# Retention states in a fused attention and MLP kernel: one scan per head pair instead of a chain of multiply-adds, with a new order of the first stage

## The chip, the cores and the metric

The kernel runs on one core of a Trainium2 chip. The metric is the device time of one execution in microseconds (us). The span of a profile is some 2 us shorter than the time of the same execution, and a profile is one execution: where it and the median of several differ, the median decides whether a kernel is faster, and the profile says where the time lies.

## The reference, cut to what matters

Four batches, 8 heads, 768 tokens, 64 elements per head. Retention keeps a 64x64 state per head, which decays by a constant gamma of that head:

```
for t in range(S):
    state = gamma * state + outer(k[t], v[t])
    y[t]  = scale * q[t] @ state
```

Its output, as 768 x 512, goes through a Fourier transform along both axes (real part), a layer norm and two dense layers (512 to 2048, relu, back to 512), with residual sums:

```
u   = x + real(fft(fft(x, axis=1), axis=2))
un  = (u - mean) / sqrt(var + 1e-6)
out = u + relu(un @ w1) @ w2
```

## The kernel before

Retention works on pairs of heads (128 partitions) and six chunks of 128 tokens. Each chunk's output has two parts. Mask products are the scores within the chunk, multiplied by a decay mask on VectorE, times v. State outputs are q times the state left by the earlier chunks. The state after chunk c is gamma^128 times the one before plus the state product kᵀv of the chunk. This is how the states are made (a matmul line of 128 x 128 holds both heads, of which the diagonal 64 x 64 blocks are used):

```python
s16 = sp.tile([P, NCH - 1, P], f16, tag="s16", name="s16")
for c0, n in ((0, 3), (3, 2)):
    wk = ps_g.tile([P, 3, P], f32, ...)                       # PSUM
    for c in range(c0, c0 + n):
        nc.tensor.matmul(wk[:, c - c0, :], kd[:, c]..., v16[:, c]..., start=True, stop=True)
    for c in range(c0, c0 + n):
        if c == 0:
            ...copy s16[:, 0] <- wk[:, 0]   # ScalarE in batch one, VectorE later
        else:
            nc.vector.scalar_tensor_tensor(out=s16[:, c], in0=s16[:, c - 1],
                scalar=gk128[:, hp:hp + 1], in1=wk[:, c - c0], op0=ALU.mult, op1=ALU.add)
```

And this is how they are used; both groups add into the same PSUM tile, state outputs first:

```python
for c in range(1, NCH):
    for h2 in range(2):
        ...lhsT = qT..., rhs = s16[..., c - 1, sl]             # 64 elements that lie together
        nc.tensor.matmul(yk[h2][:, c, :], lhsT, rhs, start=(c == 1), stop=False, ...)
for h2 in range(2):
    for c in range(NCH):
        nc.tensor.matmul(yk[h2][:, c, :], atm[:, c, h2, :], v16[:, c, h2, :], ..., stop=(c == NCH - 1))
```

Later batches' retention is interleaved with the dense layers of the batch before, so that TensorE always has large matmuls between the small ones.

## Time and profile before

| | before |
|---|---|
| median of 3 runs | 275.0 us (274.45 to 275.61) |
| span of the profile, granted clock | 273.1 us, 0.994 |
| first matmul of the first dense layer | 42.69 us |
| first and last matmul of the second dense layer | 58.36 and 268.74 us: a stretch of 210.4 us |
| state outputs in that stretch, start to start | 29 ns where they stand together; in batch two, where each uses 64 rows of TensorE, 29 ns for two, which run side by side |

The "stretch": what comes before it is the first stage, in it TensorE is almost full (busy for 201.6 of the 210.4 us in this trace). A line of a timeline has start, length, then what.

Second, TensorE's timeline (start, length, then what), at the first matmuls of the two dense layers:

```profile
42.69 4.72 PE L573 MATMUL psh<-unT,w 128*128 128x128 f16 x64
...
58.36 1.03 PE L593 MATMUL psc<-w,ht 128*128 128x512 f16 x4
```

And VectorE's, where the third batch's first pair ends. Links of the state chain and masks alternate there, and a link is last: the last state is done 1.0 us after the last mask. So it is in 13 of the 16 pairs of this trace: the last state comes after the last mask.

```profile
121.14 0.68 DVE L319 TENSOR_TENSOR atm<-wkA,maskp 128x512 f16<-128x512 f32 x1
121.74 0.34 DVE L345 SCALAR_TENSOR_TENSOR s<-s,gk,wkK 128x128 f16<-128x128 f16 x1
...
122.46 0.33 DVE L345 SCALAR_TENSOR_TENSOR s<-s,gk,wkK 128x128 f16<-128x128 f16 x1
```

### The profile page before, as it was taken

Reading aid. Unit: us, or ns where it says so; the run is one execution under the profiler, and the core shown is the slowest. Engines: PE = TensorE matmul, PEld = TensorE weight load, DVE = VectorE, ACT = ScalarE, POOL = GpSimd, SP = SyncE. Lnnn points to the kernel's source line nnn. Section 1 sums busy time; section 2 is a strip of 40 time slices with the busy share of each in tenths; the row PEclk is TensorE's granted clock in tenths of the full one; section 3 lists DMA queues with packets and bytes.
Section 4 is the critical chain, followed back from the end, with each engine's and each line's share of the span. In section 5 each row is a group of like instructions: output and inputs, shape, how many; then the busy total and the mean of one; then the engine's idle time right before and its main releaser. Section 6 shows DMA issues by size and latency. Waiting matters only on the chain.

```text
span 273.1 us, 5125 instructions
## 1 busy us (share of the span) xinstructions
PE 243.8 (89%) x1972; PEld 147.7 (54%) x1972; DVE 179.8 (66%) x458; ACT 116.6 (43%) x238; POOL 71.9 (26%) x122
## 2 busy tenths in 40 slices
PE   1498569998999998889999899989999999999994
PEld 0375458964456453556556544665566445545541
DVE  8964954986677676789778662699687736623411
ACT  3887456665554333546424540452234405402300
POOL 5769002565211214134402220510001303100000
PEclk9999997999999999999999999999999999999999
DMA  8999996999999597958996022144310131112012
GB/s 184 263 245 152 204 204 143 250 245 231 195 202 178 127 211 170 226 111 164 219 212 138 2 49 97 48 106 70 114 41 0 38 97 41 38 58 79 0 38 77
DMA packets 97432, 35.97 MB, mean 132 GB/s; under 512 B 88193, under 2 KB 94337, under 8 KB 97409
## 3 DMA queue, kind: packets, MB, share of 16 engines
q1 hardware_dynamic: 93184, 31.47, 54.2%
q0 software_dynamic: 4224, 4.19, 9.5%
q8 instruction: 15, 0.25, 0.4%
q14 instruction: 9, 0.07, 0.1%
HBM read 27.26 MB, written 6.29 MB: 123 GB/s over the span
## 4 chain that ended last, share of the span: by engine, by line
PE 56%; DVE 23%; ACT 7%; POOL 5%; issue 5%; DMA 1%; POOLq 0%; ACTq 0%; DVEq 0%
PE psc L593 25%; PE psh L556 14%; DVE bst L510 4%; PE ps L432 3%; POOL u L500 3%; PE wkY L366 2%; DVE u L491 2%; POOL u L497 2%; DVE xab L395 2%; PE tq L278 2%; PE psh L573 2%; PE wkY L370 2%; PE wkA L299 2%; DVE ht L562 2%; DVE ob L597 1%
## 5 line engine op out<-in xcount | busy, mean ns | idle before, releaser
L593 PE MATMUL psc<-w,ht 128*128 128x512 f16 x384 | 90.4, 379 | 0.7 <-DVE ht L562 0.7
L556 PE MATMUL psh<-unT,w 128*128 128x384 f16 x448 | 84.0, 326 | 0.9 <-ACT ht L560 0.5
L593 PEld LDWEIGHTS <-ht 128*128 128x128 f16 x384 | 36.0, 98 | 38.4 <-issue 2.0
L556 PEld LDWEIGHTS <-w 128*128 128x128 f16 x448 | 41.6, 98 | 27.4 <-issue 4.6
L560 ACT ACTIVATE ht<-psh 128x384 f16<-128x384 f32 x56 | 27.3, 489 | 61.6 <-PE psh L556 61.6
L562 DVE TENSOR_SCALAR ht<-psh 128x384 f16<-128x384 f32 x56 | 30.6, 547 | 11.8 <-PE psh L556 11.7
L597 DVE SCALAR_TENSOR_TENSOR ob<-psc,stats,u 128x512 f32<-128x512 f32 x24 | 17.9, 746 | 29.0 <-PE psc L593 29.0
L497 POOL TENSOR_TENSOR u<-u,x 128x256 f32<-128x256 f32 x18 | 11.5, 637 | 91.9 <-DVE u L491 89.5
L253 POOL TENSOR_SCALAR kd<-k,gexp 128x384 f16<-128x384 f32 x32 | 19.6, 623 | 30.6 <-DMA k<-in_k_dram 14.3
L512 ACT ACTIVATE un<-u,stats 128x512 f16<-128x512 f32 x21 | 15.1, 721 | 22.9 <-DVE stats L511 22.2
L378 ACT ACTIVATE x<-wkY,gexp 128x384 f16<-128x384 f32 x32 | 17.0, 585 | 16.8 <-PE wkY L370 16.7
L302 DVE SCALAR_TENSOR_TENSOR atm<-wkA,maskf 128x384 f16<-128x384 f32 x32 | 16.9, 547 | 8.7 <-PE wkA L299 8.6
L345 DVE SCALAR_TENSOR_TENSOR s<-s,gk,wkK 128x128 f16<-128x128 f16 x64 | 21.6, 338 | 0.5
L510 DVE BATCH_NORM_STATS2 bst<-u 128x6 f32<-128x512 f32 x21 | 14.6, 694 | 10.1 <-POOL u L500 9.9
L366 PE MATMUL wkY<-s,qTz 64*128 64x64 f16 (+1 forms) x160 | 16.6, 204 | 4.2 <-DVE s L345 2.9
L366 PEld LDWEIGHTS <-qTz 64*128 64x128 f16 (+1 forms) x160 | 10.7, 100 | 14.5 <-issue 9.8
L500 POOL TENSOR_TENSOR u<-u,x 128x256 f32<-128x256 f32 x21 | 13.6, 650 | 16.9 <-DVE u L493 15.7
L258 POOL TENSOR_SCALAR v<-v 128x768 f16<-128x768 f32 x16 | 13.3, 834 | 17.1 <-DMA v<-in_v_dram 7.0
L491 DVE SCALAR_TENSOR_TENSOR u<-pq,g,qn 128x257 f32<-128x257 f32 x24 | 11.5, 479 | 7.4 <-ACT qn L488 7.4
L319 DVE TENSOR_TENSOR atm<-wkA,maskp 128x512 f16<-128x512 f32 x24 | 16.3, 681 | 0.1
L573 PE MATMUL psh<-unT,w 128*128 128x128 f16 x192 | 12.7, 228 | 0.0
L573 PEld LDWEIGHTS <-w 128*128 128x128 f16 x192 | 12.2, 104 | 0.4 <-issue 0.2
(110 smaller groups left out, 294.3 us busy)
## 6 DMA issues: line engine op xcount, KB each, us to landing
q<-in_q_dram SPq DMA_DIRECT2D x16, 384.0 KB, 5.2
k<-in_k_dram SPq DMA_DIRECT2D x16, 384.0 KB, 4.9
v<-in_v_dram SPq DMA_DIRECT2D x16, 384.0 KB, 5.9
out_dram<-ob SPq DMA_DIRECT2D x24, 256.0 KB, 2.2
w<-in_moe_w_ch_dram POOLq DMA_DIRECT2D x8, 512.0 KB, 10.8
unT<-un SPq DMA_TRANSPOSE x12, 2.4
qTz<-q16z SPq DMA_TRANSPOSE x8, 3.8
kT<-kd SPq DMA_TRANSPOSE x8, 2.8
```

Source lines behind the costliest of these rows:

```text
L253: kc = nc.gpsimd.tensor_scalar(out=kd[:, :, h2, :], in0=k32[:, h2], scalar1=gkd[:, h0 + h2:h0 + h2 + 1], scalar2=1.0, op0=ALU.mult, op1=AL ...
L345: nc.vector.scalar_tensor_tensor(out=s16[:, c], in0=s16[:, c - 1], scalar=gk128[:, hp:hp + 1], in1=wk[:, c - c0], op0=ALU.mult, op1=ALU.add)
L366: nc.tensor.matmul(yk[h2][:, c, :], lhsT, rhs, start=(c == 1), stop=False, skip_group_check=True)
L378: nc.scalar.activation(dst, yk[h2], AF.Copy, bias=0.0, scale=gq8[:, h:h + 1])
L500: eng.tensor_tensor(out=u[:, kb, 256:512], in0=u[:, kb, 256:512], in1=x[:, kb, 1, 257:1:-1], op=ALU.add)
L510: nc.vector.bn_stats(bst, u[:, kb, :])
L556: nc.tensor.matmul(psh, w116[:, cb, fb * P:(fb + 1) * P], unT[:, cb, rt * 384:(rt + 1) * 384], start=(cb == 0), stop=(cb == 3))
L560: nc.scalar.activation(ht16[:, fb, :], psh, AF.Relu, bias=0.0, scale=-1.0)
L562: nc.vector.tensor_scalar(out=ht16[:, fb, :], in0=psh, scalar1=-1.0, scalar2=0.0, op0=ALU.mult, op1=ALU.max)
L573: nc.tensor.matmul(psh[:, f], w116[:, cb, fb * P:(fb + 1) * P], unT[:, cb, kb * P:(kb + 1) * P], start=(cb == 0), stop=(cb == 3))
L593: nc.tensor.matmul(psc, ht16[:, fb, rb3 * P:(rb3 + 1) * P], w216[:, fb, :], start=(fb == 0), stop=(fb == NFB - 1))
L597: nc.vector.scalar_tensor_tensor(out=ob, in0=psc, scalar=lb[b]["st"][:, rb, 3:4], in1=lb[b]["u"][:, rb, :], op0=ALU.mult, op1=ALU.add)
```

## The change

The intent: all five states of a pair by one VectorE scan (out[i] = data0[i] * out[i-1] + data1[i]). For that, the five values of one state element must lie side by side, so the products are written to PSUM with the chunk innermost, and data0 is a table of gamma^128 with zeros wherever a new element starts. A product is now made per head, as two matmuls of 64 output partitions each (column tiles), so that no unused blocks are scanned. The mask products come first and the state outputs after them, one head after the other where the two heads alternated before. The table takes room in SBUF, which is found by letting the cast queries of the first two batches share a buffer with the padded queries of the later ones; the zeroing of its padding moves from the start to the end of batch one. In the first stage the pairs are ordered so that the left half of the columns is done after two pairs, the folds that feed the transform come as soon as their heads are done, and transposes of the next pair stand ahead of the current pair's outputs. The core of the diff, with cuts:

```diff
-PAIR_ORDER = [0, 3, 1, 2]
+PAIR_ORDER = [0, 1, 3, 2]
...
+        nc.vector.tensor_copy(gk5[:, hp], gk128[:, hp:hp + 1].unsqueeze(2).to_broadcast([P, D, NCH - 1]))
+    nc.vector.memset(gk5[:, :, :, 0], 0.0)
...
-            s16 = sp.tile([P, NCH - 1, P], f16, tag="s16", name="s16")
-            ... two PSUM tiles, five matmuls of 128 columns, one copy, four multiply-adds
+            s16 = st["s16"] = sp.tile([P, D, NCH - 1], f16, tag="s16", name="s16")
+            wkf = ps_g.tile([P, D * (NCH - 1)], f32, tag="g", name="wkK", padded_shape=[P, DM])
+            wk = wkf.rearrange("p (e c) -> p e c", c=NCH - 1)
+            for c in range(NCH - 1):
+                for h2 in range(2):
+                    nc.tensor.matmul(wk[64 * h2:64 * h2 + 64, :, c], kd[:, c, h2, :],
+                                     v16[:, c, h2, :], start=True, stop=True)
+            nc.vector.tensor_tensor_scan(
+                out=s16.rearrange("p e c -> p (e c)"),
+                data0=gk5[:, hp].rearrange("p e c -> p (e c)"),
+                data1=wkf, initial=0.0, op0=ALU.mult, op1=ALU.add)
...
-            ... state outputs, rhs = s16[..., c - 1, sl], then mask products
+            ... mask products, then state outputs, rhs = s16[..., :, c - 1]
...
     def first_units():
-        un = []
+        un = [cast_unit(0, 0), tp_unit(0, 0, 0), tp_unit(0, 0, 1)]
         for i in range(4):
-            un += [cast_unit(0, i), t_unit(0, i), a0_unit(0, i, 0), kv_unit(0, i), a0_unit(0, i, 1)]
+            ... cast and transposes of pair i + 1 between a0_unit and kv_unit of pair i
...
+            if i == 1:
+                un.append(fold_s(0, 0, 258, 0, 1))
```

More of the change, by code (lines that the diff above doesn't have):

```diff
@@ L53 @@
     inp = pool("inp", 11)
-    qp = pool("qp", 2)
     vp = pool("vp", 4)
@@ L80 @@
     epsT = const.tile([P, 1], f32, tag="epsT")
-    gk128 = const.tile([P, NHP], f32, tag="gk128")
+    gk5 = const.tile([P, NHP, D, NCH - 1], f32, tag="gk5")
     pmask = const.tile([P, 4], f32, tag="pmask")
@@ L143 @@
                             scalar2=None, op0=ALU.mult)
+    gk128 = const.tile([P, NHP], f32, tag="gk128")
     for hp in range(NHP):
@@ L146 @@
         nc.vector.memset(gk128[64:128, hp:hp + 1], float(gam[2 * hp + 1] ** P))
+        nc.vector.tensor_copy(gk5[:, hp], gk128[:, hp:hp + 1].unsqueeze(2).to_broadcast(
+            [P, D, NCH - 1]))
+    nc.vector.memset(gk5[:, :, :, 0], 0.0)
     nc.gpsimd.memset(hpi, float(np.pi / 2))
@@ L154, in late_consts, with pad_unit @@
                                      scale=float(gam[h] ** (-P)))
+    def pad_unit():
         for j in range(2):
@@ L242, in run @@
                         es.enter_context(tc.issue_after(last_cast[b, i - 1].ins))
-                    q16 = qp.tile([P, NCH, 2, D], f16, tag="q16", name="q16")
+                    q16 = qzs[i % 2].rearrange("p c h t -> p (c h t)")[:, 0:NCH * P].rearrange(
+                        "p (c h d) -> p c h d", c=NCH, h=2)
                     es.enter_context(tc.issue_after(nc.gpsimd.tensor_scalar(
@@ L262, in cast_unit, with tp_unit, run @@
         return run
+    def tp_unit(b, i, part):
+        def run():
+            if part == 0:
+                at[b, i] = dict(
+                    kT=tp.tile([P, NCH, P], f16, tag="kT", name="kT"),
+                    qT=qts[i % 2].rearrange("p c h t -> p (c h) t")[:, 0:NCH])
+            st = at[b, i]
+            src = (q16_of, kd_of)[part][b, i]
+            tq = ps_g.tile([P, NCH, P], f16, tag="g", name="tq", padded_shape=[P, 8, P])
+            for c in range(NCH):
+                nc.tensor.transpose(tq[:, c, :], src[:, c].rearrange("p a b -> p (a b)"), ident16)
+            if part == 0:
+                nc.scalar.copy(st["qT"].rearrange("p c t -> p (c t)").rearrange(
+                    "p (t c) -> p t c", c=NCH), tq.rearrange("p c t -> p t c"))
+            else:
+                nc.scalar.copy(st["kT"], tq)
+        return run
@@ L264, in t_unit @@
     def t_unit(b, i):
         def run():
+            if b < NPE:
+                tp_unit(b, i, 0)()
+                tp_unit(b, i, 1)()
+                return
             st = at[b, i] = {}
             kT = st["kT"] = tp.tile([P, NCH, P], f16, tag="kT", name="kT")
-            if b >= NPE:
-                qT = st["qT"] = qts[i % 2]
-                nc.sync.dma_start_transpose(qT.rearrange("p c h t -> p (c h) t"),
-                                            q16_of[b, i].rearrange("p c h d -> p (c h d)"))
-                nc.sync.dma_start_transpose(kT, kd_of[b, i].rearrange("p c h d -> p (c h d)"))
-                return
@@ L274, in run @@
-            qT = st["qT"] = qts[i % 2].rearrange("p c h t -> p (c h) t")[:, 0:NCH]
-            for dst, src in ((qT, q16_of[b, i]), (kT, kd_of[b, i])):
-                tq = ps_g.tile([P, NCH, P], f16, tag="g", name="tq", padded_shape=[P, 8, P])
-                for c in range(NCH):
-                    nc.tensor.transpose(tq[:, c, :], src[:, c].rearrange("p a b -> p (a b)"),
-                                        ident16)
-                if dst is qT:
-                    nc.scalar.copy(dst.rearrange("p c t -> p (c t)").rearrange(
-                        "p (t c) -> p t c", c=NCH), tq.rearrange("p c t -> p t c"))
-                else:
-                    nc.scalar.copy(dst, tq)
+            qT = st["qT"] = qts[i % 2]
@@ L285, in t_unit @@
+            nc.sync.dma_start_transpose(qT.rearrange("p c h t -> p (c h) t"),
+                                        q16_of[b, i].rearrange("p c h d -> p (c h d)"))
+            nc.sync.dma_start_transpose(kT, kd_of[b, i].rearrange("p c h d -> p (c h d)"))
         return run
@@ L329, in run @@
             kd, v16 = kd_of[b, i], v16_of[b, i]
-            s16 = sp.tile([P, NCH - 1, P], f16, tag="s16", name="s16")
-            st["s16"] = s16
-            for c0, n in ((0, 3), (3, 2)):
-                wk = ps_g.tile([P, 3, P], f32, tag="g", name="wkK", padded_shape=[P, 4, P])
-                for c in range(c0, c0 + n):
-                    nc.tensor.matmul(wk[:, c - c0, :], kd[:, c].rearrange("p a b -> p (a b)"),
-                                     v16[:, c].rearrange("p a b -> p (a b)"),
-                                     start=True, stop=True)
-                for c in range(c0, c0 + n):
-                    if c == 0:
-                        if b == 0:
-                            nc.scalar.copy(s16[:, 0], wk[:, 0])
-                        else:
-                            nc.vector.tensor_copy(s16[:, 0], wk[:, 0])
-                    else:
-                        nc.vector.scalar_tensor_tensor(out=s16[:, c], in0=s16[:, c - 1],
-                                                       scalar=gk128[:, hp:hp + 1],
-                                                       in1=wk[:, c - c0],
-                                                       op0=ALU.mult, op1=ALU.add)
+            s16 = st["s16"] = sp.tile([P, D, NCH - 1], f16, tag="s16", name="s16")
[9 more added lines that the diff above has]
+                data1=wkf, initial=0.0, op0=ALU.mult, op1=ALU.add)
         return run
@@ L358, in run @@
                   for _ in range(2)]
-            for c in range(1, NCH):
-                for h2 in range(2):
-                    sl = slice(64 * h2, 64 * h2 + 64)
-                    if b < NPE:
-                        lhsT, rhs = qT[sl, c, :], s16[sl, c - 1, sl]
-                    else:
-                        lhsT, rhs = qT[:, c, h2, :], s16[:, c - 1, sl]
-                    nc.tensor.matmul(yk[h2][:, c, :], lhsT, rhs,
-                                     start=(c == 1), stop=False, skip_group_check=True)
             for h2 in range(2):
@@ L370, in run @@
                     nc.tensor.matmul(yk[h2][:, c, :], atm[:, c, h2, :], v16[:, c, h2, :],
-                                     start=False, stop=(c == NCH - 1), skip_group_check=True)
+                                     start=(c == 0), stop=False, skip_group_check=True)
+            for h2 in range(2):
+                sl = slice(64 * h2, 64 * h2 + 64)
+                for c in range(1, NCH):
+                    if b < NPE:
+                        lhsT, rhs = qT[sl, c, :], s16[sl, :, c - 1]
+                    else:
+                        lhsT, rhs = qT[:, c, h2, :], s16[:, :, c - 1]
+                    nc.tensor.matmul(yk[h2][:, c, :], lhsT, rhs, start=False,
+                                     stop=(c == NCH - 1), skip_group_check=True)
                 h = 2 * hp + h2
@@ L645, in first_units @@
     def first_units():
-        un = []
+        un = [cast_unit(0, 0), tp_unit(0, 0, 0), tp_unit(0, 0, 1)]
         for i in range(4):
-            un += [cast_unit(0, i), t_unit(0, i), a0_unit(0, i, 0), kv_unit(0, i), a0_unit(0, i, 1)]
+            nxt = i < 3
+            if nxt:
+                un += [cast_unit(0, i + 1)]
+            un += [a0_unit(0, i, 0)]
+            if nxt:
+                un += [tp_unit(0, i + 1, 0)]
+            un += [kv_unit(0, i), a0_unit(0, i, 1)]
+            if nxt:
+                un += [tp_unit(0, i + 1, 1)]
             if i == 3:
-                un += [fold_s(0, 0, 130, 0, 2), fold_s(0, 130, 258, 0, 1), fold_d(0, 0),
-                       g0_unit(0), s1_unit(0, 0, 0), s1_unit(0, 1, 0)]
+                un += [fold_s(0, 0, 130, 1, 2), fold_d(0, 0), g0_unit(0), s1_unit(0, 0, 0),
+                       s1_unit(0, 1, 0)]
             un.append(y_unit(0, i))
+            if i == 1:
+                un.append(fold_s(0, 0, 258, 0, 1))
             if i < 3:
@@ L656, in first_units @@
                 un.append(parity_consts)
-        un += [xmean_unit(0), fold_s(0, 130, 258, 1, 2), fold_d(0, 1), s1_unit(0, 0, 1),
-               s1_unit(0, 1, 1), xmean_unit(1), xmean_unit(2), mean_unit]
+        un += [fold_s(0, 130, 258, 1, 2), fold_d(0, 1), s1_unit(0, 0, 1), s1_unit(0, 1, 1),
+               xmean_unit(0), xmean_unit(1), xmean_unit(2), mean_unit]
         return un
@@ L716 @@
             streams.append((mix_units(b + 1, [0, 1, 2]), b + ts[-1], b + ts[-1] + 0.15))
+    streams.append(([pad_unit], 0.9, 0.95))
     emit(streams)
```

## The prediction

> **What bounds the kernel now.** I read the page first, then the stages, then the matmuls of one stage in order of time, then the first stage engine by engine.
>
> The page's busy time (first block), then busy time by stage (us from the start; busy us and count of each engine, granted clock, DMA share, GB/s):
>
> ```profile
> PE 243.8 (89%) x1972; PEld 147.7 (54%) x1972; DVE 179.8 (66%) x458; ACT 116.6 (43%) x238; POOL 71.9 (26%) x122
> ```
> ```profile
> 20.00:30.00 10.00, 7.72 (x88) 5.27 (x87) 5.60 (x15) 6.53 (x14) 7.27 (x11) 1.00 1.09 171
> ...
> 180.00:210.00 30.00, 29.79 (x270) 18.72 (x269) 24.68 (x63) 10.45 (x22) 1.23 (x2) 1.00 0.30 69
> 210.00:240.00 30.00, 28.64 (x160) 15.38 (x159) 17.28 (x40) 11.15 (x24) 7.39 (x12) 1.00 0.18 49
> ```
>
> There are two regimes. From about 62 us on TensorE is nearly full, so an instruction counts there only by the TensorE time it takes or makes TensorE wait. Before 43 us no engine is full: it is a chain of loads, casts, copies and small vector operations for the first batch, ending when the first dense layer starts at 42.7 us.
>
> The groups the change touches (busy us, mean ns of one, idle before and its releaser):
>
> ```profile
> L345 DVE SCALAR_TENSOR_TENSOR s<-s,gk,wkK 128x128 f16<-128x128 f16 x64 | 21.6, 338 | 0.5
> ...
> L302 DVE SCALAR_TENSOR_TENSOR atm<-wkA,maskf 128x384 f16<-128x384 f32 x32 | 16.9, 547 | 8.7 <-PE wkA L299 8.6
> L319 DVE TENSOR_TENSOR atm<-wkA,maskp 128x512 f16<-128x512 f32 x24 | 16.3, 681 | 0.1
> ...
> L366 PE MATMUL wkY<-s,qTz 64*128 64x64 f16 x80 | 9.1, 215 | 1.7 <-DVE s L345 1.7
> ...
> L335 PE MATMUL wkK<-v,kd 128*128 128x128 f16 x80 | 8.3, 241 | 0.0
> ...
> L366 PE MATMUL wkY<-s,qTz 128*128 128x64 f16 x80 | 7.5, 192 | 2.6 <-DVE s L345 1.2 <-DVE s L343 0.8 <-DVE unT L543 0.2
> ```
>
> The second batch (64 to 74 us, TensorE's timeline) shows what pieces cost, from start to start:
>
> ```profile
> 63.36 0.82 PE L593 MATMUL psc<-w,ht 128*128 128x512 f16 x3
> 64.11 0.20 PE L366 MATMUL wkY<-s,qTz 64*128 64x64 f16 x1
> 64.24 0.39 PE L593 MATMUL psc<-w,ht 128*128 128x512 f16 x1
> ...
> 69.74 0.44 PE L335 MATMUL wkK<-v,kd 128*128 128x128 f16 x5
> 70.02 1.03 PE L593 MATMUL psc<-w,ht 128*128 128x512 f16 x4
> ...
> 73.33 0.52 PE L370 MATMUL wkY<-v,atm 128*128 128x64 f16 x12
> 73.69 1.24 PE L593 MATMUL psc<-w,ht 128*128 128x512 f16 x5
> ```
>
> Twelve L370 take 0.36 us, 30 ns each with a 128-column weight load in it. Five L335 take 0.28 us, 56 ns each. In long runs L593 comes every 0.216 us, so three are 0.65; here the next start, a matmul of 64 rows, is at 0.75: 0.10 us lost on entering the 64-row form. It then takes 0.13 us instead of 0.03: 0.10 lost on leaving. State by state, as VectorE delivers them, these matmuls are scattered between large ones.
>
> The first stage, last pair of heads (ACT copies the transposed key, PE multiplies, DVE masks and makes states):
>
> ```profile
> 25.16 0.80 ACT L284 COPY kT<-tq 128x768 f16<-128x768 f16 x1
> ```
> ```profile
> 26.01 0.39 PE L299 MATMUL wkA<-qTz,kT 64*128 64x128 f16 x4 [0.72 <-ACT kT L284]
> ...
> 30.97 0.24 PE L366 MATMUL wkY<-s,qTz 64*128 64x64 f16 x2 [0.50 <-DVE s L345]
> ...
> 33.40 1.13 PE L432 MATMUL ps<-csp,eo 128*128 128x193 f16 x6
> ...
> 37.23 0.64 PE L482 MATMUL pq<-cd,g 128*128 128x257 f16 x2
> ```
>
> POOL, second batch's second pair:
>
> ```profile
> 55.64 1.15 POOL L253 TENSOR_SCALAR kd<-k,gexp 128x384 f16<-128x384 f32 x2 [0.73 <-DMA k<-in_k_dram]
> ```
>
> This key is cast at 56.8 us, straight behind its load, and TensorE transposes it at 58.0: 1.2 us of slack, which limits what an earlier start can bring.
>
> [...]
>
> **The change part by part.**
>
> States. Removed per pair: five matmuls of 128 columns (0.28 us) and the chain of four L345 plus one copy. From start to start an L345 takes about 0.25 us, so the chain costs VectorE some 1.2 us, and spread among other work it took 3.3 us for the pair at 63 us. Added: ten matmuls with 64 output partitions and 64 columns, written every fifth fp32, and one scan of 320 elements. The mask rows above give the full rate: 512 elements take 681 ns, 384 take 547, so 1.05 ns per element. [...] The larger effect is on waits: TensorE's waits in front of L366 from 62 us on add up to some 3.5 us. Not all go, as the mask products are now needed first and VectorE still finishes them after the scan. I count 2.5: 0.5 in batch two, 2.0 in three and four.
>
> State products. At the rate of L370 ten would again take 0.29 us[...]. Then the mode: batches three and four have no switches now and get two per pair, 8 x 2 x 0.10 = 1.6 us. In batch two the new instruction order has its state products in one run instead of among large ones. Counting changes of mode in the orders of both, all from the first dense layer on go from 56 to 53; 16 of the 53 are the new ones of batches three and four, so batch two goes from 56 to 37: 19 x 0.10 = 1.9 us saved; I take 1.7.
>
> State outputs. The ten L366 per pair now read the state every fifth element. I allow 0 to 24 ns each, up to double time: 120 x 10 ns as a mean is 1.2 us (0.4 and 0.8).
>
> First stage. Four 0.26 us copies of the first state leave ACT; transposes of the next pair are issued before the current pair's outputs; four fills of the decay table come at the start of VectorE (about 1.2 us) while 0.8 us of zeroing leaves it. ACT was continuously busy from 14.3 to 23.8 us, and its trigonometric tables stand ahead of the last key copy in both orders. Adding the copies in the new order, I get that key at 24.5 to 25.9 us against 25.96 before. What surely goes is the chain behind it: two masks 1.0, [...]two masks 0.95 put the last mask near 28.5, against 30.8 for the last state now. The left fold is then done, and the first half of the transform runs beside the last outputs, so the L482 at 37.2 should come at about 34: 3.2 us earlier.
>
> That isn't all kept. The second batch's loads wait for the last weights and don't move. The key cast at 56.8 us holds the transpose that would come at 54.8. From there four L593, six score matmuls and nine L593 (about 3.6 us with switches) follow; the transpose behind them at 62.5 us can move to 60.4. I keep 2.0 us.
>
> Sum in us: first stage -2.0; batch two -0.5 +0.5 -1.7 +0.4 = -1.3; batches three and four -2.0 +1.1 +1.6 +0.8 -0.3 = +1.2; total -2.1. From 275.0 that is 272.9. I go to 272.3, as the allowances for strides are guesses and cautious ones.
>
> **The rivals.** A: column tiles run side by side, stride costs nothing, most waits vanish: product and stride terms go to 0 and a further 1 us of waits is saved, about 269. For it: the 64-row pairs of batch two already overlap. B: [...]24 ns per output matmul, while waits only change their name to masks: against the sum above that is +1.4, +1.7 and +2.5, total 278.5. For it: masks are last on VectorE in both orders. C: the first stage gains nothing because ACT delivers the last key no earlier and folds wait there: 274.9. Against it: the 4 us after the key lie on VectorE. D: the load doesn't hold the second batch, since TensorE catches up: 271.7.
>
> **Range and chances.** A with D is 268, and B by half is 275.7: these ends hold most of it. Two per cent is below 269.5, which needs A nearly whole. Slower than 280.5 needs several errors of one sign. So 268 to 275.5; faster 0.2, same 0.77, slower 0.03.
>
> **What would show it.** Right: the L482 start near 34 us; TensorE waiting for the second pair's key in batch two; [...]waits for states gone[...]. Wrong: [...]output matmuls near 29 ns (no stride cost) or over 60; waits of the same length now ending on mask products; or the first dense layer not earlier by 2 us.

The sum came to -2.1 us, and from 272.9 to 272.3 us. Three of its terms stand in it as numbers only: +0.5 and +1.1 for the time of ten state products, and -0.3 for VectorE's time with the scan. Without them the terms left come to -3.4 us. A's 269 and B's +1.4 hold the product terms too, and the last mask near 28.5 us and the L482 near 34 us hold an allowance for the scan. The 0 to 24 ns for the strided read and the fills' 1.2 us were guesses of mine, from no trace (measured later: 44 ns more, 1.8 us).

A change of mode, here and below, is one between matmuls of 128 rows and 128 output partitions and those that use 64 of either. The 0.10 us each way was measured for 64 rows; for 64 output partitions it was an estimate. The later traces agree with it: four large matmuls, 0.86 us by themselves, and the change took 0.97 us ahead of the changed kernel's ten products (68.45 to 69.42), against 0.88 ahead of the five of 128 columns (68.86 to 69.74 before); and behind them, with contiguous outputs, the next start came after 130 ns instead of about 30 (e10). That the second batch's loads wait for the weights is in the trace before: the queue stood 27.8 us for a weight's transfer and issued the first of these loads at 44.68 us (28.6 and 45.27 in the changed kernel).

## More of the kernel before

The prediction shows most lines. Three more are needed later. First, the group of mask products (busy us, mean ns of one, then idle time before them; TensorE never sat idle in front of one):

```profile
L370 PE MATMUL wkY<-v,atm 128*128 128x64 f16 x192 | 9.5, 205 | 0.0
```

## The result, and the profile after

The changed kernel takes 281.6 us (280.81 to 282.36, 4 runs) against 275.0 (274.45 to 275.61, 4 runs): slower, ratio 1.024 with an interval of 1.020 to 1.028. A ratio here is the mean time of one kernel's runs over that of the other's in the same rounds, so not quite the ratio of the medians quoted. The profiled execution was the fastest of the four, with a span of 278.8 us, 5.7 more than before, at the same clock (0.993).

The page's busy line:

```profile
PE 249.1 (89%) x2052; PEld 152.4 (55%) x2052; DVE 173.9 (62%) x403; ACT 116.4 (42%) x234; POOL 72.1 (26%) x122
```

VectorE lost 5.9 us of work, as intended, and TensorE got 5.3 us more: near the size of the loss. The first matmuls of the dense layers:

```profile
42.02 5.36 PE L580 MATMUL psh<-unT,w 128*128 128x128 f16 x64
...
58.25 1.03 PE L600 MATMUL psc<-w,ht 128*128 128x512 f16 x4
```

The second dense layer starts 0.1 us earlier than before and ends at 274.39, 5.7 later. So the first stage brought nothing, and the whole loss lies in the stretch, which is 216.1 us instead of 210.4. The groups there:

```profile
L368 PE MATMUL wkY<-v,atm 128*128 128x64 f16 x192 | 15.0, 205 | 5.1 <-DVE atm L317 2.3 <-DVE atm L334 1.5 <-DVE s L352 1.1
...
L352 DVE TENSOR_TENSOR_SCAN s<-gk,wkK 128x320 f16<-128x320 f32 x16 | 13.0, 812 | 3.9 <-PE wkK L350 3.9
...
L350 PE MATMUL wkK<-v,kd 128*64 128x64 f16 x160 | 8.6, 270 | 0.0
L377 PE MATMUL wkY<-s,qTz 64*128 64x64 f16 x80 | 8.3, 244 | 0.0
...
L377 PE MATMUL wkY<-s,qTz 128*128 128x64 f16 x80 | 7.2, 251 | 0.0
```

The state outputs (L377) have no wait left; before (L366) they had 1.7 and 2.6 us. But the mask products, which had none, now have 5.1. And one state output lasts 244 to 251 ns instead of 192 to 215. Those are overlapping durations; what counts is from start to start, which the timeline of the second batch shows:

```profile
69.42 0.47 PE L350 MATMUL wkK<-v,kd 128*64 128x64 f16 x10
69.82 1.04 PE L600 MATMUL psc<-w,ht 128*128 128x512 f16 x4
```

Ten products take 0.40 us up to the next large matmul; before, five took 0.28. In the third batch's first pair both effects stand beside each other:

```profile
120.22 0.22 PE L368 MATMUL wkY<-v,atm 128*128 128x64 f16 x2 [0.84 <-DVE s L352]
...
121.34 0.29 PE L368 MATMUL wkY<-v,atm 128*128 128x64 f16 x4 [0.57 <-DVE atm L334]
...
122.13 0.90 PE L377 MATMUL wkY<-s,qTz 128*128 128x64 f16 x10
122.85 0.40 PE L492 MATMUL pq<-sd,g16r 128*128 128x255 f16 x2
```

First TensorE waits in front of mask products, by the profile for the scan and then for a mask; then ten state outputs take 122.85 - 122.13 = 0.72 us, about 73 ns each. VectorE's timeline of the same time says why it waits: the scan was done at 120.17, the last two masks at 121.88. In all 16 pairs of the changed kernel the scan is done 0.9 to 2.1 us before the last mask.

```profile
119.37 0.80 DVE L352 TENSOR_TENSOR_SCAN s<-gk,wkK 128x320 f16<-128x320 f32 x1
...
120.60 1.28 DVE L334 TENSOR_TENSOR atm<-wkA,maskp 128x512 f16<-128x512 f32 x2
```

Summing start to start from the first second-dense-layer matmul on: state outputs 9.39 us (before 6.30, waits in it), mask products 7.34 (4.28), products 4.83 (3.45). That is 7.5 us more, where the stretch grew by 5.7: the second dense layer's own matmuls, between which fewer state outputs are scattered, took 2.0 less (86.4 against 88.5). TensorE's idle time within the stretch was 2.6 us in front of state outputs before, and is 2.8 in front of mask products now.

In the first stage, VectorE's fills of the decay table, of which two more (0.56 us) stand between these lines:

```profile
1.66 0.96 DVE L147 COPY gk<-gk 128x320 f32<-128x320 f32 x2
...
3.84 0.27 DVE L149 MEMSET gk<- 128x256 f32 x1 [0.31 <-DVE gk L147]
```

The trigonometric arguments that follow them start at 5.30 us instead of 3.47, and the first mask at 14.07 instead of 12.11. The last key copy is at 27.64 us instead of 25.16.

### The profile page after: what moved, and what is told of

It is laid out like the page before. It is cut to its first block, busy times and chain, and to the rows that moved or that the text cites. A ratio compares the mean times of both kernels' runs of the same rounds, so it can differ in the third digit from the quotient of the medians. Undisturbed runs are those within 1.5% of the kernel's fastest.

```text
span 278.8 us, 5231 instructions
## 1 busy us (share of the span) xinstructions
PE 249.1 (89%) x2052; PEld 152.4 (55%) x2052; DVE 173.9 (62%) x403; ACT 116.4 (42%) x234; POOL 72.1 (26%) x122
## 4 chain that ended last, share of the span: by engine, by line
PE 39%; DVE 8%; POOL 4%; ACT 3%; issue 1%; DMA 1%; POOLq 0%; ACTq 0%
PE psc L600 23%; PE psh L563 10%; DVE bst L517 3%; POOL u L507 2%; PE wkY L377 2%; POOL u L504 1%; DMA qTz<-q16z 1%; DVE ht L569 1%; PE wkY L368 1%; DVE atm L334 1%; PE wkA L332 1%; DVE s L352 1%; DVE u L498 1%; PE ps L439 1%; ACT ht L567 1%
## 5 line engine op out<-in xcount | busy, mean ns | idle before, releaser
L600 PE MATMUL psc<-w,ht 128*128 128x512 f16 x384 | 89.5, 379 | 1.1 <-DVE ht L569 0.7
L563 PE MATMUL psh<-unT,w 128*128 128x384 f16 x448 | 82.7, 326 | 1.6 <-DVE ht L569 0.9
L563 PEld LDWEIGHTS <-w 128*128 128x128 f16 x448 | 42.4, 98 | 27.4 <-issue 2.8
L385 ACT ACTIVATE x<-wkY,gexp 128x384 f16<-128x384 f32 x32 | 17.8, 584 | 18.7 <-PE wkY L377 17.9
L368 PE MATMUL wkY<-v,atm 128*128 128x64 f16 x192 | 15.0, 205 | 5.1 <-DVE atm L317 2.3
L317 DVE SCALAR_TENSOR_TENSOR atm<-wkA,maskf 128x384 f16<-128x384 f32 x32 | 16.3, 545 | 4.2 <-PE wkA L314 4.1
L368 PEld LDWEIGHTS <-atm 128*128 128x128 f16 x192 | 10.7, 103 | 13.1 <-DVE atm L317 4.3
L377 PE MATMUL wkY<-s,qTz 64*128 64x64 f16 (+1 forms) x160 | 15.5, 248 | 0.0
L352 DVE TENSOR_TENSOR_SCAN s<-gk,wkK 128x320 f16<-128x320 f32 x16 | 13.0, 812 | 3.9 <-PE wkK L350 3.9
L580 PE MATMUL psh<-unT,w 128*128 128x128 f16 x192 | 13.3, 235 | 0.1
```

The lines of the kernel that those rows point to most:

```text
L377: nc.tensor.matmul(yk[h2][:, c, :], lhsT, rhs, start=False, stop=(c == NCH - 1), skip_group_check=True)
L385: nc.scalar.activation(dst, yk[h2], AF.Copy, bias=0.0, scale=gq8[:, h:h + 1])
L563: nc.tensor.matmul(psh, w116[:, cb, fb * P:(fb + 1) * P], unT[:, cb, rt * 384:(rt + 1) * 384], start=(cb == 0), stop=(cb == 3))
L600: nc.tensor.matmul(psc, ht16[:, fb, rb3 * P:(rb3 + 1) * P], w216[:, fb, :], start=(fb == 0), stop=(fb == NFB - 1))
```

## The experiments

My theory after the trace: (1) state outputs are slow because they read every fifth element; (2) the waits only changed their name; (3) the fills took the first stage's gain. Rivals: the time is lost to the column tiles and their changes of mode, to the new order of the outputs, or to the new first stage itself. The runs, with first second-dense-layer matmul and stretch from each one's profile:

| run | median us (range) | ratio to before | first, us | stretch, us |
|---|---|---|---|---|
| before | 275.0 (274.45 to 275.61) | | 58.4 | 210.4 |
| after | 281.6 (280.81 to 282.36) | 1.024 | 58.3 | 216.1 |
| e1 before, strided states | 283.6 (282.11 to 284.62) | 1.031 | 59.5 | 218.0 |
| e2 after, GpSimd copies states to rows | 285.1 (283.97 to 285.97) | 1.036 | 63.9 | 214.2 |
| e3 after, old first stage | 285.2 (284.35 to 286.9) | 1.038 | 60.4 | 217.8 |
| e4 before, new first stage | 274.9 (274.5 to 275.03) | 1.000 | 58.0 | 210.4 |
| e5 before, masks first | 280.0 (279.42 to 282.34) | 1.020 | 62.8 | 210.4 |
| e6 before, states 8 bytes apart | 278.8 (277.69 to 278.96) | 1.014 | 57.3 | 214.3 |
| e7 after, states read in rows (wrong) | 277.7 (276.23 to 278.86) | 1.009 | 59.2 | 213.1 |
| e8 after, fills on GpSimd | 279.9 (279.42 to 280.27) | 1.017 | 57.1 | 217.1 |
| e9 after, states first | 277.8 (276.45 to 278.26) | 1.008 | 57.7 | 214.2 |
| e10 after, products in rows (wrong) | 279.5 (279.26 to 280.55) | 1.017 | 57.3 | 215.5 |
| e11 before, masks first, new first stage | 275.9 (275.59 to 278.41) | 1.004 | 59.2 | 212.8 |
| e12 after, fills and rows mended | 279.0 (278.24 to 279.69) | 1.013 | 57.9 | 215.4 |
| e13 after, states first, fills on GpSimd | 276.4 (275.91 to 276.73) | 1.004 | 56.3 | 214.3 |
| e14 after, states first, rows (wrong) | 275.4 (275.15 to 276.06) | 1.001 | 57.2 | 211.8 |
| e15 before, products per head | 280.7 (278.62 to 281.97) | 1.018 | 65.1 | 210.1 |
| e16 e15 with new first stage | 275.8 (275.23 to 275.8) | 1.001 | 60.4 | 209.3 |
| e17 scan in batch one only | 274.0 (273.24 to 274.44) | 0.996 | 56.9 | 209.9 |

Kernels marked wrong give wrong values. The changed kernel was not run again beside these, so a comparison with it goes across rounds; the kernel before was, and its medians stayed between 275.1 and 275.5 us. And a stretch is that of one execution: the changed kernel's profile is its fastest run, those of e9 and e11 are their slowest. Two further edits did not build, so nothing was learned from them on the chip: a scan whose operands were three-dimensional views (the build refused it, so in the correct kernels here the scan neither writes rows nor reads products from rows), and padding all five states to 8 bytes (no room in SBUF).

### The stride of the states: e1, e6, e7

e1 puts the kernel before's states five elements apart and changes nothing else:

```diff
-s16 = sp.tile([P, NCH - 1, P], f16, ...)
+s16 = sp.tile([P, P, NCH - 1], f16, ...)    # and every use s16[.., c, ..] -> s16[.., .., c]
```

> The kernel before with one thing of the change: its state tile laid out so that a state's elements lie five apart, as the scan leaves them. Theory (the strided read of the state costs TensorE about 44 ns per output matmul): in the trace the state matmuls of batches three and four go from 29 to about 73 ns, and the time from 275 to 279 or 280. Rival (the loss of the change comes from mode switches of the new products and from waits that only changed their name): it stays at 275 to 276.

The strided layout costs the kernel before 8.5 us: 283.6, more than I expected, and slower than the whole change. In batches three and four state outputs take 50 to 80 ns, with a median of 73 as in the changed kernel. But this layout is not only read by TensorE. VectorE writes and reads the chain of states with the same stride, and one link took 563 ns instead of 338; the idle time in front of state outputs in the stretch rose from 2.6 to 4.6 us. TensorE's reads are an estimated 3.5 us (37 ns more on average for 80 outputs, 29 for each of batch two's 20 pairs) of the 7.6 us by which the stretch grew; 1.1 us lie in the first stage. So e1 can't say what the reads alone cost. e7 can, as it leaves VectorE's work as it was, and it goes the other way, in the changed kernel: the state outputs read 64 elements that lie together (the wrong ones).

```diff
-rhs = s16[sl, :, c - 1]
+rhs = s16.rearrange("p e c -> p (e c)")[sl, D * (c - 1):D * c]
```

> The changed kernel, whose output matmuls read 64 contiguous elements of the scanned tile: the values are wrong on purpose, all else is as in the change. Theory (the stride alone explains the loss): state matmuls at 29 ns, 275.5 to 277, so 5 to 6 us less than the changed kernel. Rival (products, switches and moved waits carry half of the loss): 278 to 280.

State outputs are back at 29 ns, their sum in the stretch is 4.33 us instead of 9.39, and the time falls by 3.9 us, to between the two ranges: the stride is the largest part of the loss and not all of it. The group rows of e7, to be held against the same two rows after:

```profile
L377 PE MATMUL wkY<-s,qTz 64*128 64x64 f16 x80 | 6.1, 215 | 0.0
...
L377 PE MATMUL wkY<-s,qTz 128*128 128x64 f16 x80 | 3.6, 193 | 0.0
```

e6 sets four of the five states 8 bytes apart in the kernel before:

```diff
-s16 = sp.tile([P, NCH - 1, P], f16, tag="s16", name="s16")
+s16t = sp.tile([P, (NCH - 1) * P], f16, tag="s16", name="s16")
+s4 = s16t[:, 0:4 * P].rearrange("p (e c) -> p e c", c=4)
+s16 = [s4[:, :, 0], s4[:, :, 1], s4[:, :, 2], s4[:, :, 3], s16t[:, 4 * P:]]
```

> The kernel before with four of its five states four elements (8 bytes) apart instead of five, the fifth contiguous. [...]state matmuls at 29 ns and 275 to 276. Rival[...]: 73 ns and 281 to 283.

That 8 bytes would cost nothing was an idea which no run had shown, and so was the rival's, that they cost what 10 bytes do. Neither came true: with states at 8 bytes a state output that followed another took some 60 ns (the first of a run some 40), against 29 in rows and 73 at 10 bytes. The kernel became 1.4% slower, to which VectorE's chain adds its part here too (453 ns a link against 338). So for the kernel at hand the states have to lie together.

### Getting the rows back: e2, e12

The scan as built does not write rows, so its result has to be copied. e2 lets GpSimd do it, e12 VectorE (with the fills on GpSimd as well):

```diff
+sec = sp.tile([P, D, NCH - 1], f16, tag="sec", name="sec")       # the scan writes here
+nc.gpsimd.tensor_copy(s16, sec.rearrange("p e c -> p c e"))      # e12: nc.vector
```

> The changed kernel, but GpSimd copies the scanned states into rows of 64 contiguous elements before TensorE reads them. Theory of the strided read: output matmuls go back to 29 ns and the time to 276 or 277, a little less of it if the copy comes late for TensorE. Rival (switches and waits): 281 or more, as the copy adds latency.

Missed, by 8 us; the rival's range holds it. The state outputs did come back to 29 ns and the stretch fell to 214.2, but the copies stand in GpSimd's queue ahead of its weight loads' issues: the last four are issued from 34.5 us on instead of 24.9, the second batch's keys arrive later, and TensorE waits for their casts, twice some 1.6 us (at 58.5 and 63.6 us in e2's timeline).

> The changed kernel mended in its two shown faults, correct results: VectorE copies each scanned state into rows of 64 elements that lie together, so that the state outputs read them without a stride, and the decay table is filled by GpSimd. Theory (stride 5.3 us, fill 1.7 us of the loss): state outputs 29 ns each again, total 276 to 278.5, since the copies lengthen VectorE's work by about 0.4 us per pair, which the mask products then wait for in part. Rival one (the copy's delay costs all that the stride cost): 279.5 or more. Rival two (nothing of the copy is on the path): below 275.

279.0: half a microsecond above the range, and only 2.6 better than the changed kernel, less than e7 gained with the row layout alone. The copy takes 0.51 us of VectorE ahead of the last masks, and the mask products' sum grew from 7.34 to 8.16 us.

### The first stage: e3, e4, e8

e3 gives the changed kernel the old order of the first stage, e4 gives the kernel before the new one.

```diff
-PAIR_ORDER = [0, 1, 3, 2]      # e3; e4 the reverse
+PAIR_ORDER = [0, 3, 1, 2]      # with first_units() and the transposes' grouping of that kernel
```

> The changed kernel with the first batch's order of before (order of pairs, transposes, folds). Theory (what the new first order wins is gone by 58 us, because the second batch's start doesn't move): 281 to 282.5, with the second dense layer starting within 0.7 us of 58.3. Rival (the new order is still worth 2 us in the end): 283.5 or more.

> The kernel before with the first batch's new order alone (pair order, early transposes, early folds), its states unchanged. Theory (the order wins 1 to 2 us at the start of the first dense layer when no table fills delay VectorE, but the second batch's loads[...] eat it): first dense layer at 41 to 42 us, total 274 to 275. Rival (the order itself is worth 2 us): 273 or less.

e3 is slower than the changed kernel by 3.6 us, which the theory missed and the rival had, so the new order is not what lost the time; within the changed kernel it helps. In the kernel before it wins nothing (ratio 1.000, interval 0.996 to 1.003): 0.4 us at the second dense layer. e8 moves the fills to GpSimd:

```diff
-nc.vector.tensor_copy(gk5[:, hp], ...);  nc.vector.memset(gk5[:, :, :, 0], 0.0)
+nc.gpsimd.tensor_copy(gk5[:, hp], ...);  nc.gpsimd.memset(gk5[:, :, :, 0], 0.0)
```

> The changed kernel with its decay table filled by GpSimd instead of VectorE. Theory (the fills delay VectorE's tables and the first masks by some 2 us, and that is why the new first order won only 0.7 us): first mask near 12.5 us instead of 14.1 and the first dense layer 1 us earlier, at 41 us; in the total 0 to 1 us, as the second batch's loads don't move: 280.5 to 281.6. Rival (later waits decide the first stage): first dense layer at 42 us or later.

The first dense layer starts at 40.84 us, 1.2 earlier, and the kernel is 1.7 us faster, more than expected. So the fills on VectorE did delay the first stage. But not as I thought: the first mask came at 13.79 us instead of 14.07, not near 12.5. Of the 2.0 us by which it is late, e8 removes 0.3; what holds the rest, and by what path the 1.2 us were won, is not shown.

### The order of the two groups: e5, e9, e11, e14

e5 puts the kernel before's mask products ahead of its state outputs; e11 does so together with the new first stage.

```diff
-for c ...: for h2 ...: state output (start=(c == 1))
-for h2 ...: for c ...: mask product (stop=(c == NCH - 1))
+for h2 ...: for c ...: mask product (start=(c == 0))
+for h2 ...: for c ...: state output (stop=(c == NCH - 1))
```

> The kernel before with the change's order of output matmuls alone: mask products first, then each head's states in one run. Theory of the prediction (fewer changes of TensorE's mode in batch two are worth 1.7 us, and fewer waits for states 2 us more): 271 to 273. Rival (the wait only moves to the masks, which VectorE finishes last): 274.5 to 276.

> The kernel before with the new order of the first stage and with mask products ahead of state outputs, that is the whole change without the scan, the column-tiled products and the decay table. Theory (neither order wins or loses anything in the steady stretch; what the changed kernel lost is all in how states are made and laid out): 274 to 276, the stretch of second dense layers 210.4 within 1. Rival (part of the loss comes from the orders together): 277 or more.

Both ranges of e5 were missed. Its stretch is the same as before to 0.1 us, so there, with the chain of states, this order neither wins nor costs. e5's 5 us lie in the first stage, which the order reshuffled: TensorE was granted half its clock from 41.6 to 48.4 us (before: 41.3 to 44.7; 64 matmuls of the first dense layer took 5.89 us there, and 3.73 at full clock), and waited 1.8 us for a copy of the normalized rows. e11, where the first stage has its new order, is 1 us above e4. Its stretch missed the expected range by 1.4 us. In it TensorE had a half-clock window from 60.2 to 63.6 us, where the others have none; but of the 2.4 us over e4's stretch, 1.6 come after 129 us, at full clock. It is the profile of e11's slowest run (278.4, the others 275.6 to 276.0), so whether masks first cost the chain up to 1 us stays open. e9 is the mirror image: the changed kernel with states first.

> The changed kernel with the output matmuls in the old order again, state outputs ahead of mask products, while scan, strided states and new first stage stay. Theory (the waits in front of the state outputs were not removed by the scan, the mask products put first only took them over, since mask products need what VectorE finishes last): waits go back in front of the state outputs, the sum of both groups from the first to the last second dense layer matmul stays within 1 us of the changed kernel's, and the stretch stays at 216 us within 1; total 280.5 to 283. Rival (the new order of the two groups is itself what costs, since a state is ready before the last mask): the stretch falls by 2 us or more, total below 280.

My theory fell here: 277.8, 3.8 us better than the changed kernel. The profiles, of a slow run of e9 and a fast one of the changed kernel, show 2.6 of it: 0.6 up to the second dense layer and 2.0 in the stretch. The same pair as above, in e9's timeline of TensorE:

```profile
117.38 0.89 PE L373 MATMUL wkY<-s,qTz 128*128 128x64 f16 x10 [0.90 <-DVE s L352]
118.09 0.73 PE L377 MATMUL wkY<-v,atm 128*128 128x64 f16 x8
```

The state outputs start as the scan ends, and TensorE does all ten while VectorE makes the last two masks. In the changed kernel they came after those masks. Over equal work, from four large matmuls ahead of the pair to the large ones behind it, e9 takes 4.20 us here (115.66 to 119.86) and the changed kernel 4.57 (118.52 to 123.09).

That is not where most of the gain lies, though. Over the stretch the waits only moved: the idle time in front of the two groups together is 2.8 us in the changed kernel, all of it ahead of mask products, and 2.9 in e9, nearly all of it ahead of state outputs. What became shorter is batch two. Its second pair, in the changed kernel and then in e9 (left out in the first: one large matmul and three mask products):

```profile
71.94 0.55 PE L368 MATMUL wkY<-v,atm 128*128 128x64 f16 x9
72.42 0.52 PE L377 MATMUL wkY<-s,qTz 64*128 64x64 f16 x5
...
73.29 0.52 PE L377 MATMUL wkY<-s,qTz 64*128 64x64 f16 x5
73.74 1.68 PE L600 MATMUL psc<-w,ht 128*128 128x512 f16 x7
```
```profile
70.66 0.58 PE L373 MATMUL wkY<-s,qTz 64*128 64x64 f16 x10
71.18 0.52 PE L377 MATMUL wkY<-v,atm 128*128 128x64 f16 x12
71.54 1.89 PE L600 MATMUL psc<-w,ht 128*128 128x512 f16 x8
```

The pair takes 1.57 us in the changed kernel (1.80 less the one large matmul between, 0.23) and 0.88 in e9. With masks first the ten state outputs are split, five of one head and later five of the other, and the five follow each other at 73 ns, with a change of mode before and after. In e9 all ten stand together, and most of them run two side by side, a pair in some 73 ns. For all four pairs of batch two the two groups take 6.4 us from start to start in the changed kernel, 3.7 in e9 and 4.3 before.

Why did the order not matter in e5? Its state outputs lie in rows: batch two's groups take 4.6 us there with masks first, against 4.3 before. And its states come one by one between the masks and mostly end last, so there is no whole group of state outputs that could run ahead. The scan makes all states ready 1.7 us before the last mask in the pair shown (120.17 against 121.88), and masks first throws that lead away. This reading rests on the traces; no run shifted the lead by itself, or changed the grouping of the heads by itself. e14 asks whether this order also hides the stride, with e9's and e7's edits together:

> The changed kernel with state outputs first and with each read at 64 elements that lie together (wrong values on purpose). Theory (with states first, TensorE does the slow strided state outputs while VectorE finishes the last masks, so their stride is hidden behind a wait that would be there anyway): like states first alone, 277.8, at most 1.3 us less, with the mask products' waits longer by what the state outputs save. Rival (stride and wait simply add, in either order): 274.8 or less.

The result, 275.4, lies between the two theories: it is 2.4 us below e9, where e7 won 3.9 with masks first (by the stretches, 2.3 and 3.0). So a part of the stride's cost is hidden and the larger part adds. The hidden part is again in batch two: there the stride adds 1.7 us to the two groups with masks first (6.4 against e7's 4.7) and 0.6 with states first (3.7 against 3.1); in batches three and four together it adds 3.0 and 2.8. Together the two edits win 6.2 us and leave the changed kernel as fast as before (ratio 1.001, interval 0.999 to 1.002). The stretch is still 1.5 us longer than before (211.84 against 210.38), about what the products grew by, and a first stage that is 1.1 us shorter makes up for it.

### The products: e10, e15, e16

e10 writes each product of the changed kernel to 64 PSUM elements that lie together, instead of every fifth.

```diff
-nc.tensor.matmul(wk[64 * h2:64 * h2 + 64, :, c], ...
+nc.tensor.matmul(wkf[64 * h2:64 * h2 + 64, D * c:D * c + D], ...
```

> The changed kernel, but each state product is written to 64 elements of PSUM that lie together instead of every fifth one; the scan then reads them in the wrong order and the result is wrong on purpose. Theory (the strided write of PSUM costs nothing, what is slow in the products is the change of mode in and out of the column tiles, plus about 25 ns per matmul): ten products still take about 0.25 us with their two switches of 0.1 to 0.15, the group's sum from the first second dense layer on stays at 4.8 us within 0.2, total within 1 us of the changed kernel (280.6 to 282.6). Rival (the stride in PSUM slows them): the sum falls by 1 us or more, total 280.5 or less.

The theory fell, the stride in PSUM does cost: ten products up to the next large matmul take 0.28 us instead of 0.40, and the group's sum fell from 4.83 to 3.35 us. From start to start a pair of column tiles took about 56 ns in the changed kernel and about 29 in rows, in three cases of four; the last pair was left 0.05 us sooner. This is e10's timeline:

```profile
68.36 0.35 PE L350 MATMUL wkK<-v,kd 128*64 128x64 f16 x10
68.64 1.04 PE L600 MATMUL psc<-w,ht 128*128 128x512 f16 x4
```

Of the 1.5 us, 0.6 arrived in the stretch. The time fell by 2.1, of which some 1 us comes from an earlier first stage. e15 puts per-head products into rows in the kernel before and keeps the chain, on 64 columns instead of 128; e16 has the new first stage besides.

```diff
-nc.tensor.matmul(wk[:, c - c0, :], kd[:, c]..., v16[:, c]..., start=True, stop=True)
+for h2 in range(2):
+    nc.tensor.matmul(wk[64 * h2:64 * h2 + 64, c - c0, :], kd[:, c, h2, :], v16[:, c, h2, :], start=True, stop=True)
```

> The kernel before with the column-tiled products per head alone: ten products of 64 columns to contiguous PSUM, the chain of multiply-adds kept but on 64 columns instead of 128, states in rows without a stride. Theory (changes of mode in and out of column tiles cost about 0.1 us each, contiguous products 16 ns each, and the halved chain saves VectorE about 0.06 us per link, which is not on the path): products' sum from the first second dense layer on 3.3 to 3.5 us, as many mode switches more as in the changed kernel counted in; total 274.5 to 276.5. Rival (the shorter chain shortens TensorE's waits for states): 273.5 or less.

> The same with the changed kernel's order of the first stage as well: the whole change less the scan, its decay table, its strided layout and the masks-first order. Theory: 274 to 276, no better than the kernel before within 1 us. Rival (first stage now keeps its gain, as no fills stand before it and the chain is halved): 273 or less.

The products' sum is 3.35 us in both, and the stretches, 210.1 and 209.3 us, are as short as before's or shorter. So per-head products in column tiles are not the cause of the loss; their stride is a small part of it. e15's time missed its range because its first stage went wrong in the way of e5's (half clock from 51.7 to 58.5 us, 4 us of waits for copies of normalized rows from 50 us on). In e16 the first stage waited 2.3 us for a fold.

### What the first stage can give: e13, e17

e13 is e9 with the fills on GpSimd.

> The changed kernel with state outputs ahead of mask products again and the decay table filled by GpSimd; correct results. If the two repairs (3.8 us and 1.7 us, each measured alone) add: 276.0, range 275 to 277.3. If the earlier first stage is taken up by a later wait: 277.3 or more. Below 274.5 would beat the kernel before, and neither theory expects it.

276.4, as expected. Its TensorE timeline is what the prediction had in mind for the first stage: the transform (L489 there) starts at 34.22 us, the first dense layer at 39.58 and the second at 56.30.

e17 takes each stage from where it was best: scan, GpSimd fills and states first in batch one; e16's chain into rows with per-head products in batches two to four.

```diff
+def kv_unit(b, i):
+    return kv_scan_unit(b, i) if b == 0 else kv_chain_unit(b, i)
```

> Scan, strided states and GpSimd fill for the first batch alone (where TensorE is not full), with the new order of the first stage and state outputs first; in batches two to four per-head products to contiguous PSUM and the chain of multiply-adds into rows of 64, in the old order of outputs. Correct results. If each stage keeps what it did in the kernel where it was best: the first second dense layer at 56.3 us as with the order and fill mended, then 209.3 us as with per-head products, and 4.4 us to the end of the span: 270.0 for the profiled span, 270.5 to 272 for the median. If an earlier first stage is taken up by a later load or wait, or the gains of the first stage belong to the profiled run alone: 273 to 275.

274.0 us and correct, ratio 0.996 (interval 0.994 to 0.998): the only version that beats the kernel before, by less than half a per cent. The medians' range of 270.5 to 272 was missed. The profiled run comes near the sum that I made (span 271.2 instead of 270.0; second dense layer 0.6 us later than in e13, stretch 0.5 longer than in e16), but it was the fastest of six.

## Why the prediction was wrong

Point by point, in the order of its sum:

- **State outputs, the step that failed.** It allowed "0 to 24 ns each, up to double time" and took 10, 1.2 us in all. Measured: 73 ns against 29, and 5.1 us for the 120 matmuls of the stretch (9.39 against 4.33 in e7), 42 each. The mechanism was named and the size was off by more than four times. e7 shows that the stride is the cause, 3.9 us of time in the changed kernel.
- **Waits, the second failing step.** The -2.5 us did not come: TensorE's idle time in front of the two groups was 2.6 us of the stretch and is 2.8. Rival B had the words ("waits only change their name to masks") and the size. But its reason, "masks are last on VectorE in both orders", was wrong for the kernel before, whose chain of states ends after the masks in 13 of 16 pairs (122.46 against 121.14 us in the pair shown). In the changed kernel the masks are last, and the new order makes ten state outputs wait for them though their states are ready.
- **The order of the outputs in batch two.** The prediction gave it only a gain, 1.7 us of fewer changes of mode. The traces have as many changes from the first dense layer on as it counted, 56 before and 53 after. But it knew that "the 64-row pairs of batch two already overlap", and had no cost for splitting them: the two groups of batch two take 6.4 us instead of 4.3. e9, which brings them together again and puts the ready states first, is 3.8 us faster; how much each of the two is worth was not separated.
- **State products.** +1.6 us for the products and +1.6 for the new switches in batches three and four, less 1.7 in batch two: +1.5 net. The group's sum, which holds the switch behind it and not the 0.09 us ahead of it, rose by 1.4; batch two's saving was not measured by itself. The size was about right, for a wrong reason: two column tiles run side by side (starts 3 and 53 ns apart), so ten matmuls are done in about 0.25 us, less than I had allowed. What costs is the strided write to PSUM, 1.5 us by e10, which I had left without a number.
- **Scan.** 0.81 us measured for 320 elements, where a mask took 0.68 for 512; my estimate was near. VectorE's 5.9 us less work bought nothing directly, nearly as predicted (-0.3 in the sum).
- **First stage.** -2.0 us predicted as kept, -0.1 measured. The transform was to start near 34 us and started at 36.58. The last key, put at 24.5 to 25.9 us, was copied by 28.4. Two causes were left out or undersized: fills counted as 1.2 less 0.8 us (they took 1.8; without them on VectorE, e8 starts the first dense layer 1.2 us earlier), and masks first, which delayed the pairs here too (e9 starts it 1.4 us earlier). With both taken out, e13 gives 34.22 us for the transform, 3.1 us at the first dense layer, and 2.1 kept at the second. So the argument held and its inputs didn't.
- **The rivals and the chances.** B's 278.5 was the nearest. With the measured stride in place of its 24 ns, B would have said 281 (20 ns more for 120 matmuls, 2.4 us). Giving slower than 2% a chance of 0.03 was the error of judgement: three guessed terms, of which all could be larger and one was only bounded from an idea ("double time"), do not leave such a narrow upper end.

What stays open: why the first stage reacts to small edits by up to 7 us (e5, e15). Their traces show half-clock windows and waits behind a changed order, but no run separated the two. And e15 to e17 don't say which of the first stage's waits sets the 56 to 57 us at which the second dense layer seems to be held: in e13 it waits 0.5 us for a key cast there.

## What to carry to other kernels

When a vector rewrite changes a layout, price the matmuls that read it and write it first, by their start-to-start time in the trace, and measure one before trusting an allowance: a stride of five took these from 29 to 73 ns. When two groups of matmuls wait for the same vector engine, try first the order in which their inputs are ready, and look again whenever the vector work changes its order; look also at which small matmuls then stand together, as pairs that ran side by side may be split. A fill at the start of a latency-bound stage is not free, even where the engine looks half idle on average: taking 1.8 us of them off VectorE won 1.7 us here.
